# Sliding-window attention and an MLP on one core: a mask built on VectorE, key chunks shared by two query blocks, and a reordered, repacked load of the first batch

## The chip, the core and the metric

The kernel runs on one core of a Trainium2 chip. The metric is the device time of one execution in microseconds (us), as the median of several runs; smaller is better.

## What is computed

The first stage is attention over 8 batches, 8 heads, 576 tokens and 64 values per head, where a token sees the tokens at most 32 away from it. The second stage is an MLP on the 4608 tokens, 512 wide, with 2048 hidden values.

```python
scores = scale * np.matmul(q, k.transpose(0, 1, 3, 2))
mask = np.abs(pos[:, None] - pos[None, :]) <= 32
scores = np.where(mask, scores, -1000000000.0)
attn = softmax(scores)
x = np.matmul(attn, v).transpose(0, 2, 1, 3).reshape(4608, 512)
h = x @ w_in                       # 512 -> 2048
g = h * (1.0 / (1.0 + np.exp(-1.702 * h)))
out = (g @ w_out).astype(np.float32)
```

## The kernel before

**Tiling.** The 4608 tokens are cut into 36 units of 128 query tokens, and two units make one tile `t` of 256 tokens for the MLP. For a unit `u`, `scores` (L230) makes two PSUM tiles `sc`, one for the even and one for the odd heads. Each unit needs 192 keys, that is three chunks of 64; each of its two blocks of 64 queries uses two of them. A product has 64 contracted values, 64 keys and 64 queries, so it fills one quarter of the array, and four different quarters follow one another: per head pair 2 blocks x 2 key halves x 2 (even, odd) = 8 products, 32 in a unit. ScalarE takes the exponential (L251). In the first four units the window is cut before that by `blind` (L222), which puts -30000 into `sc` with a product of the identity and the tile `neg`; later units multiply by a 0/1 mask on VectorE (`band`, L254). `values` (L265) multiplies by v with a column of ones, `norm` (L278) divides on VectorE (4 instructions), `x_T` (L289) transposes the result into `xT`, on TensorE in the first eight units and by a DMA later. A unit's second block needs v shifted by 64 tokens: `odd_v` (L163) makes that copy `vo` with two instructions, the second of which needs the first half of the next unit's v.

**MLP.** `layer1(t, d)` (L304) makes two of 16 hidden blocks (8 products 128x256, w_in first), and ScalarE takes the activation. Column quarter `c` of w_in serves `d` = 2c and 2c+1. The second layer follows in the window after (`layer2` for the first tiles, then `product`, `keep` and `result` with sums made by `g_sums` and `w_sums`).

**Order.** The schedule is manual: each engine executes its instructions in the order in which the Python code calls them, and only semaphores tie the engines together. `head` (L421) writes out the order of the first four units and of all first loads; `window` (L578) does the rest, one window of 14.6 us for each later pair of units.

**Loads.** k, q, v and the weights are 32-bit in DRAM and are cast on the way, so all but the first four loads are issued by GpSimd (POOL) on one queue, which the DMA engines serve in order. A load's issue also waits until the eighth load before it on this queue has landed. The first batch's k and q come in two parts, since a part is what is needed first: part A is tokens 0 to 319 (two head pairs raw through SP and ACT, the others by POOL), part B tokens 320 to 575. Part B lies on 64 partitions with 4 tokens of a head in a row of 1 KB of source; VectorE pairs two heads (`pair_heads`, L200), TensorE transposes 4 times per head pair, and VectorE (k) or ScalarE (q) copies the result into the rings `kT` and `qT` (`rows_T`, L186).

**The order of POOL's work before** is: ident; k and q of part A; `neg` (one memset, four selects); v of units 0, 1, 2; k and q of part B; v 3; half of v 4; four quarters of w_in; `odd_v` of units 2 and 3 (four copies); w_out 0 and 2; the mask (9 instructions); k and q of tokens 512 to 1023 ("batch 1" below); w_out 1; more v.

**The order of TensorE before**, after the part A transposes, is: scores 0 and 1; 3 junk products; values 0; 3 junk; x_T 0; 1 junk; values 1; 4 junk; x_T 1; blind 2 and 3; 1 junk; the part B transposes; scores 2 and 3; layer1(0,0); values 2; layer1(0,1); values 3; x_T 2; layer1(0,2); x_T 3; layer1(0,3); layer1(1,0) and on. The junk products (`keep_busy`, L414) write nothing that is used.

Of the kernel before, what the change touches and what calls it, by code (L numbers as in the profile page):

```python
# [16 lines left out]
BF16 = mybir.dt.bfloat16  # L17
F16 = mybir.dt.float16
AF = mybir.ActivationFunctionType
ALU = mybir.AluOpType  # L20

SQ = 64
JT = 4
NV = 8
RING = 1536


class _Kernel:
# [7 lines left out]
    def __init__(self, ctx, tc, q, k, v, w_in, w_out, out):  # L36
        self.tc, self.nc = tc, tc.nc
        self.q, self.k, self.v, self.w_in, self.w_out, self.out = q, k, v, w_in, w_out, out
        self.B, self.H, self.S, self.D = q.shape
        self.N = self.B * self.S  # L40
        self.DM = self.H * self.D
        self.DFF = w_in.shape[1]
        self.NK = self.DM // 128
        self.NFF = self.DFF // 128
        self.scale = 1.0 / (self.D ** 0.5)
        self.NU = self.N // 128
        self.NW = self.NU // 2

        def pool(name, bufs, **kw):
            return ctx.enter_context(tc.tile_pool(name=name, bufs=bufs, **kw))  # L50

        self.cst = pool("cst", 1)
        self.work = pool("work", 2)
        self.ps = pool("ps", 1, space=bass.MemoryType.PSUM)
        self.stage, self.paired = {}, set()
        self.span = {"A": (0, 320), "B": (320, 256)}
        self.xT, self.g, self.o_ps = {}, {}, {}
        self.p, self.acc, self.x, self.sc = {}, {}, {}, {}
        self.gs, self.part, self.o_sb = {}, {}, {}
# [94 lines left out]
            self.nc.sync.dma_start_transpose(dst[:, :, at:at + 128],  # L154
                                             self.stage[c, i][:, n].rearrange("p h d -> p (h d)"))

    def load_v(self, m, half=None):
        for i, (off, b, s, n) in enumerate(self.pieces(128 * m, 128)):
            if half in (None, i):
                self.nc.gpsimd.dma_start(self.ve[m % NV][off:off + n, :, :self.D],  # L160
                                         self.v[b, :, s:s + n, :].rearrange("h s d -> s h d"))

    def odd_v(self, m, eng):  # L163

# [21 lines left out]
    def rows_T(self, c, i, hp, kind, eng):  # L186
# [3 lines left out]
        self.cast(eng, dst[:, hp, at:at + size].rearrange("r (p j) -> r p j", j=JT),  # L190
                  tp[:, :, :size // JT].rearrange("r j p -> r p j"))

    def load_raw(self, c, hp, eng):

        lo, size = self.tokens("A")
        raw = self.stage[c, "raw", hp] = self.cst.tile([size // JT, 2, JT * self.D], F32, name=f"{c}_raw{hp}")
        src = {"q": self.q, "k": self.k}[c]
        eng.dma_start(raw, src[0, 2 * hp:2 * hp + 2, lo:lo + size, :].rearrange("h (p j) d -> p h (j d)", j=JT))
# [10 lines left out]

    def setup_neg(self):  # L210

        pool = self.nc.gpsimd
        self.neg = self.cst.tile([128, 2, SQ], BF16, name="neg")
        pool.memset(self.neg, 0.0)
        for b in range(2):
            for half in range(2):
                sign = 1 if half == b else -1
                ap = self.neg[64 * half:64 * half + 64, b, :]
                pool.affine_select(out=ap, in_=ap, compare_op=ALU.is_ge, fill=-30000.0, base=0,  # L219
                                   pattern=[[-sign, SQ]], channel_multiplier=sign)  # L220

    def blind(self, u):  # L222

# [6 lines left out]
    def scores(self, u):  # L230
        nc = self.nc
        seen = u not in self.sc
        if seen:
            self.sc[u] = [self.bank("a", [128, 8, SQ], F32, f"sc{eo}") for eo in range(2)]
        sc = self.sc.pop(u)
        n = 0
        for hp in range(4):
            for blk in range(2):
                k0 = (128 * u + 64 * blk) % RING
                q0 = (128 * u + 64 * blk + 32) % RING  # L240
                for half in range(2):
                    lo, at = 64 * half, k0 + 64 * (half ^ blk)
                    for eo in range(2):
                        r = slice(eo * 64, eo * 64 + 64)
                        nc.tensor.matmul(sc[eo][lo:lo + 64, 2 * hp + blk, :], self.kT[r, hp, at:at + 64],  # L245
                                         self.qT[r, hp, q0:q0 + SQ], start=(seen and n == 0),
                                         stop=(n == 7), skip_group_check=not seen)
                n += 1
        p = self.work.tile([128, 2, 8, SQ], BF16, name="p", tag="p", bufs=5)
        for eo in range(2):  # L250
            nc.scalar.activation(p[:, eo], sc[eo], AF.Exp, scale=self.scale)  # L251
        self.p[u] = p
# [168 lines left out]
    def head(self):  # L421

        nc, dve, act, pool = self.nc, self.nc.vector, self.nc.scalar, self.nc.gpsimd
# [4 lines left out]
        for c in "kq":  # L428
            self.load_heads("A", c, (4, 8))
        self.setup_neg()  # L430
        for m in range(3):
            self.load_v(m)
        for c in "kq":
            self.load_heads("B", c)
        self.load_v(3)
        self.load_v(4, 0)
        for c in range(4):
            self.load_w_in(c)
        self.odd_v(2, pool)
        self.odd_v(3, pool)  # L440
        for c in (0, 2):
            self.load_w_out(c)
        self.setup_mask()
        self.cut_mask()
        for c in "kq":
            self.load_heads(1, c)
        self.load_w_out(1)
        self.load_v(4, 1)
        for m in range(5, 7):
            self.load_v(m)  # L450
        self.load_w_out(3)
# [12 lines left out]
        self.scores(0)  # L464
        self.scores(1)
        self.odd_v(0, dve)
        self.odd_v(1, act)
        self.keep_busy(3, "h")
        self.values(0, "hh")
        self.norm(0)  # L470
        self.keep_busy(3, "o")
        self.x_T(0, "t", act)
        self.keep_busy(1, "o")
        self.values(1, "oa")
        self.norm(1)
        self.keep_busy(4, "a")
        self.x_T(1, "a", act)
        self.blind(2)
        self.blind(3)
        self.keep_busy(1, "h")  # L480
        for hp in range(4):
            self.pair_heads("k", "B", hp, dve)
        for hp in range(2):
            self.pair_heads("q", "B", hp, dve)
        for hp in range(4):
            self.rows_T("k", "B", hp, "htho"[hp], dve)
            if hp < 2:
                self.pair_heads("q", "B", hp + 2, dve)
            self.rows_T("q", "B", hp, "hoth"[hp], act)
        self.scores(2)  # L490
        self.scores(3)
        self.layer1(0, 0)
        self.values(2)
        self.norm(2)
        self.layer1(0, 1)
        self.values(3)
        self.norm(3)
        self.x_T(2, "t")
# [274 lines left out]
```

## Time and profile before

| what | value |
|---|---|
| median of 5 runs | 294.05 us (293.83 to 295.7) |
| the profiled execution | 293.83 us, span of its instructions 292.1 us |
| TensorE busy | 285.6 us, 98% of the span |
| VectorE, ScalarE, GpSimd busy | 187.7, 185.2, 104.3 us |
| time before the first layer1 product starts its unbroken run (L313) | 18.69 us |
| 128x256 products of layer 1, one after another | 109 ns each |
| scores of two units, 64 products | 0.67 us |

The profile counts time from the first instruction. A line of a timeline or of the chain begins with start and length in us. The chain of work that ended last is followed back from the end, at each step to what released the step. TensorE's products overlap, so one product's length (193 ns for a scores product) is not the time between two of them.

The trace also has the moment at which a load's semaphore was complete, for most of the first loads:

```
load               issued us    landed us
k A, q A           1.57, 2.36   6.58, 7.39
v 0, 1, 2          4.35 to 7.17 -, 9.78, 10.80
k B, q B           7.15, 7.83   -, 14.72
v 3, half of v 4   8.51, 9.38   15.78, 16.12
w_in 0, 1, 2, 3    10.05 to 13.1  18.45, -, 23.53, 26.08
w_out 2            18.57        31.16
k batch 1 (last)   21.99        33.86
```

### The profile page before, as it was taken

To read this page: it belongs to the slowest core of one execution; us is meant where nothing else is said; L and a number is where in the kernel's file an instruction comes from. 1 tells how busy PE (TensorE), PEld (TensorE's weight loads), DVE (VectorE), ACT (ScalarE), POOL (GpSimd) and SP (SyncE) were. 2 spreads that over 40 slices of the span, in tenths; PEclk is the share of its full clock that TensorE was granted. 3 is DMA by queue.
4 is the path that set the end of the run, shared out by engine and by line. 5 is a ranking of instruction groups with operands and counts; after the bars stand their busy time and mean duration, and the time that the engine had idled before them with its cause. 6 is when DMAs were issued, how large, how long until landed. Compare 5 with 4: busy or idle time off the path is not lost.

```text
span 292.1 us, 9542 instructions
## 1 busy us (share of the span) xinstructions
PE 285.6 (98%) x4020; PEld 235.0 (80%) x4020; DVE 187.7 (64%) x552; ACT 185.2 (63%) x306; POOL 104.3 (36%) x146
## 2 busy tenths in 40 slices
PE   8989999999999999999999999999999999999995
PEld 3568764866888888888888888887888888888884
DVE  2663367688485858585858585857585858583353
ACT  4677547685766767676767676766575757575330
POOL 8875534989634444342424443332000000000000
PEclk9999999999999999999999999999999999999999
DMA  8999999999999999999999999999925330303012
GB/s 145 153 206 206 200 184 166 172 135 151 163 156 173 155 143 156 160 139 199 126 165 128 179 107 151 142 162 130 162 43 143 41 105 8 104 10 103 2 72 72
DMA packets 145291, 38.83 MB, mean 133 GB/s; under 512 B 129888, under 2 KB 140896, under 8 KB 145248
## 3 DMA queue, kind: packets, MB, share of 16 engines
q0 software_dynamic: 97696, 18.16, 85.1%
q1 hardware_dynamic: 47104, 19.67, 40.1%
q8 instruction: 31, 0.51, 0.7%
q10 hardware_dynamic: 448, 0.39, 0.5%
q14 instruction: 12, 0.10, 0.1%
HBM read 36.96 MB, written 9.44 MB: 159 GB/s over the span
## 4 chain that ended last, share of the span: by engine, by line
PE 93%; DVE 2%; DMA 2%; POOL 1%; issue 1%; ACT 0%; POOLq 0%; DVEq 0%
PE h_ps L313 43%; PE o_ps L375 32%; PE o_ps L325 7%; PE pv L273 4%; PE sc L245 4%; DMA ve<-in_v_dram 2%; PE tp L179 1%; PE tp L300 1%; DVE x L285 1%; PE sc L227 0%; POOL ve L160 0%; DVE o_sb L393 0%; POOL neg L219 0%; DVE kT L105 0%; ACT qT L105 0%
## 5 line engine op out<-in xcount | busy, mean ns | idle before, releaser
L313 PE MATMUL h_ps<-xT,w_in_sb 128*128 128x256 bf16 x1152 | 135.1, 273 | 0.0
L315 ACT ACTIVATE g<-h_ps 128x512 f16<-128x512 f32 x144 | 85.5, 595 | 73.9 <-PE h_ps L313 72.6
L313 PEld LDWEIGHTS <-w_in_sb 128*128 128x128 bf16 x1152 | 112.1, 98 | 13.3
L160 POOL DMA_DIRECT2D ve<-in_v_dram x40 | 34.0, 856 | 78.0 <-PE pv L273 57.9
L375 PEld LDWEIGHTS <-gs 128*128 128x128 f16 x480 | 45.8, 98 | 5.8
L375 PE MATMUL o_ps<-w_sum,gs 128*128 128x256 f16 x360 | 44.3, 273 | 0.0
L251 ACT ACTIVATE p<-sc 128x512 bf16<-128x512 f32 x72 | 37.2, 603 | 2.7 <-PE sc L245 2.5
L375 PEld LDWEIGHTS <-g 128*128 128x128 f16 x360 | 34.2, 98 | 4.5 <-ACT g L315 0.2
L352 DVE TENSOR_TENSOR gs<-g 128x512 f16<-128x512 f16 x30 | 12.7, 425 | 38.3 <-ACT g L315 38.3
L285 DVE TENSOR_TENSOR x<-pv,rec 128x256 bf16<-128x256 f32 x72 | 30.6, 425 | 2.5
L375 PE MATMUL o_ps<-w_out_sb,g 128*128 128x256 f16 x240 | 29.1, 273 | 0.0
L105 DVE COPY part<-o_ps 128x256 f32<-128x256 f32 x45 | 19.1, 424 | 13.3 <-PE o_ps L375 11.8
L393 DVE TENSOR_TENSOR o_sb<-o_ps,part 128x256 f32<-128x256 f32 x45 | 19.0, 423 | 12.0 <-PE o_ps L375 11.4
L147 POOL DMA_DIRECT2D qs<-in_q_dram x27 | 22.9, 869 | 5.7 <-DMA ks<-in_k_dram 4.3
L262 DVE TENSOR_TENSOR p<-p,mask 128x512 bf16<-128x512 bf16 x64 | 24.5, 424 | 0.6 <-ACT p L251 0.5
L147 POOL DMA_DIRECT2D ks<-in_k_dram x27 | 22.8, 860 | 2.1 <-DMA ve<-in_v_dram 2.1
L325 PE MATMUL o_ps<-w_out_sb,g 128*128 128x512 f16 x96 | 23.2, 380 | 0.0
L105 DVE COPY vo<-ve 64x528 bf16<-64x528 bf16 x65 | 20.7, 318 | 2.8 <-DMA ve<-in_v_dram 1.4
L251 ACT ACT_TABLE_LOAD x15 | 19.2, 1283 | 0.3
L412 ACT ACT_TABLE_LOAD x15 | 19.2, 1283 | 0.3
L284 DVE RECIPROCAL rec<-pv 128x4 f32<-128x4 f32 x72 | 12.6, 175 | 10.3 <-PE pv L273 10.3
L273 PEld LDWEIGHTS <-p 128*64 128x64 bf16 x576 | 11.2, 110 | 6.6 <-DVE p L262 3.2
(70 smaller groups left out, 246.8 us busy)
## 6 DMA issues: line engine op xcount, KB each, us to landing
out_dram<-o_sb SPq DMA_DIRECT2D x34, 256.0 KB, 6.1
ve<-in_v_dram POOLq DMA_DIRECT2D x32, 128.0 KB, 6.0
ks<-in_k_dram POOLq DMA_DIRECT2D x22, 128.0 KB, 7.9
qs<-in_q_dram POOLq DMA_DIRECT2D x22, 128.0 KB, 9.7
w_in_sb<-in_moe_w_in_dram POOLq DMA_DIRECT2D x4, 512.0 KB, 12.0
w_out_sb<-in_moe_w_out_dram POOLq DMA_DIRECT2D x4, 512.0 KB, 12.6
ve<-in_v_dram POOLq DMA_DIRECT2D x8, 64.0 KB, 5.6
ks<-in_k_dram POOLq DMA_DIRECT2D x7, 64.0 KB, 6.2
```

What stands on the lines that cost most here:

```text
L105: (eng.copy if eng is self.nc.scalar else eng.tensor_copy)(out, in_)
L147: self.nc.gpsimd.dma_start(self.stage[key][off:off + m, n], src[b, :, s:s + m, :].rearrange("h s d -> s h d"))
L160: self.nc.gpsimd.dma_start(self.ve[m % NV][off:off + n, :, :self.D], self.v[b, :, s:s + n, :].rearrange("h s d -> s h d"))
L251: nc.scalar.activation(p[:, eo], sc[eo], AF.Exp, scale=self.scale)
L262: self.nc.vector.tensor_mul(pv, pv, msk.to_broadcast([128, 4, 2, SQ]))
L273: nc.tensor.matmul(acc[half][blk * 64:blk * 64 + 64, hh, :], p[:, h % 2, h // 2 * 2 + blk, :], vt[:, h, :D + 1], start=(hh == 0), stop=(hh ...
L285: nc.vector.tensor_mul(x[:, hs, :], acc[half][:, :, :D], rec[:, hs, :].to_broadcast([128, 4, D]))
L313: nc.tensor.matmul(hps[:, i, :], self.w_in_sb[:, kr, ff * 128:(ff + 1) * 128], self.xT[t][:, kr, :], start=(i == 0 and kr == 0), stop=(i = ...
L315: nc.scalar.activation(self.g[t][:, ffs[0]:ffs[1] + 1:ffs[1] - ffs[0], :], hps, AF.Gelu_apprx_sigmoid)
L325: nc.tensor.matmul(o_ps, self.g[t][:, ff, s * 128:(s + 1) * 128], self.w_out_sb[:, ff, :], start=(ff == 0), stop=(ff == self.NFF - 1))
L375: nc.tensor.matmul(self.part[t, key], x, y, start=(first and k == 0), stop=(k == 7), skip_group_check=True)
L412: self.nc.scalar.activation(self.spark, self.spark, AF.Gelu_apprx_sigmoid)
```

## The change

- `neg` is made by 14 small VectorE instructions (running sums of the identity, then scale and shift) in place of POOL's 5.
- v 2 and v 4 are loaded in halves of 64 tokens; only the first half of v 2 stands ahead of part B.
- Part B is loaded by `load_rest`: rows of 8 tokens of a head (2 KB of source), heads 0 to 3 on partitions 0 to 31 and heads 4 to 7 on 32 to 63, so four loads in place of two. `rest_T` transposes it without pairing, 32 products of 64x64 for k and 32 for q into one PSUM tile each, and two copies of 128x512 per tile, one by ScalarE and one by VectorE. The built program makes the second copy of each tile wait for the first.
- The first quarter of w_in is issued behind part B, ahead of the rest of v 2, of v 3 and of v 4.
- `odd_v` of unit 1 goes from ScalarE to VectorE, those of units 2 and 3 from POOL to VectorE, behind scores 3.
- `scores`: the middle key chunk takes both query blocks in one product of 128 columns, so a head pair has 6 products, 24 in a unit. The columns streamed are as many as before.
- Order: x_T 0 and 1 now stand behind values 1, between the part B transposes of k and of q; blind 3 stands behind those; layer1(0,1) stands ahead of values 2; there are 5 junk products fewer; the loads of batch 1 are issued ahead of the mask.

```diff
+    def load_rest(self, c):
+        rest = self.stage[c, "B"] = self.work.tile([128, 4, 8 * self.D], BF16, name=c + "s", tag=c + "s", bufs=3)
+        src = {"q": self.q, "k": self.k}[c]
+        for g in range(2):
+            self.nc.gpsimd.dma_start(rest[32 * g:32 * g + 32],
+                                     src[0, 4 * g:4 * g + 4, 320:576, :].rearrange("h (p j) d -> p h (j d)", j=8))
+    def rest_T(self, c, kind, engs):
+        tp = self.bank(kind, [128, 2, 8, 64], BF16, "tp")
+        for n in range(4):
+            for j in range(8):
+                self.nc.tensor.transpose(tp[64 * (n % 2):64 * (n % 2) + 64, n // 2, j, :],
+                                         self.stage[c, "B"][:64, n, j * self.D:(j + 1) * self.D], self.ident[:64, :64])
+        dst = {"q": self.qT, "k": self.kT}[c]
+        for g in range(2):
+            self.cast(engs[g], dst[:, 2 * g:2 * g + 2, 320:576].rearrange("r h (p j) -> r h p j", j=8),
+                      tp[:, :, :, 32 * g:32 * g + 32].rearrange("r h j p -> r h p j"))
...
-        pool.memset(self.neg, 0.0)
-        for b in range(2):
-            for half in range(2):
-                sign = 1 if half == b else -1
-                ap = self.neg[64 * half:64 * half + 64, b, :]
-                pool.affine_select(out=ap, in_=ap, compare_op=ALU.is_ge, fill=-30000.0, base=0,
-                                   pattern=[[-sign, SQ]], channel_multiplier=sign)
+        for i in range(2):
+            dve.memset(tri[i][:, :pad], 0.0)
+        for rows in (lo, hi):
+            dve.tensor_copy(tri[0][rows, pad:], self.ident[rows, rows])
+        for i in range(6):
+            a, b = tri[i % 2], tri[(i + 1) % 2]
+            dve.tensor_add(b[:, pad:], a[:, pad:], a[:, pad - (1 << i):pad + SQ - (1 << i)])
+        for rows, b in ((lo, 0), (hi, 1)):
+            dve.tensor_scalar(out=self.neg[rows, b, :], in0=tri[0][rows, pad - 1:pad + SQ - 1], scalar1=-30000.0,
+                              scalar2=None, op0=ALU.mult)
+            dve.tensor_scalar(out=self.neg[rows, 1 - b, :], in0=tri[0][rows, pad:], scalar1=30000.0, scalar2=-30000.0,
+                              op0=ALU.mult, op1=ALU.add)
...
+            for chunks in ((1, 0), (2,)):
+                for eo in range(2):
+                    r = slice(eo * 64, eo * 64 + 64)
+                    for c in chunks:
+                        lo = 64 * (c % 2)
+                        b0, n = (1, 1) if c == 2 else (0, 1 + c)
+                        nc.tensor.matmul(sc[eo][lo:lo + 64, 2 * hp + b0:2 * hp + b0 + n, :],
+                                         self.kT[r, hp, k0 + 64 * c:k0 + 64 * c + 64],
+                                         self.qT[r, hp, q0 + SQ * b0:q0 + SQ * (b0 + n)],
...
-        for m in range(3):
+        for m in range(2):
             self.load_v(m)
-        for c in "kq":
-            self.load_heads("B", c)
+        self.load_v(2, 0, 64)
+        for c in "kq":
+            self.load_rest(c)
+        self.load_w_in(0)
+        self.load_v(2, 64)
         self.load_v(3)
-        self.load_v(4, 0)
-        for c in range(4):
+        self.load_v(4, 0, 64)
+        for c in range(1, 4):
             self.load_w_in(c)
-        self.odd_v(2, pool)
-        self.odd_v(3, pool)
         for c in (0, 2):
             self.load_w_out(c)
+        for c in "kq":
+            self.load_heads(1, c)
         self.setup_mask()
         self.cut_mask()
-        for c in "kq":
-            self.load_heads(1, c)
...
-        self.odd_v(1, act)
+        self.odd_v(1, dve)
         self.keep_busy(3, "h")
         self.values(0, "hh")
         self.norm(0)
-        self.keep_busy(3, "o")
-        self.x_T(0, "t", act)
-        self.keep_busy(1, "o")
+        self.keep_busy(2, "o")
         self.values(1, "oa")
         self.norm(1)
-        self.keep_busy(4, "a")
-        self.x_T(1, "a", act)
         self.blind(2)
+        self.rest_T("k", "t", (act, dve))
+        self.x_T(0, "h", act)
+        self.x_T(1, "h", act)
+        self.rest_T("q", "o", (dve, act))
         self.blind(3)
-        self.keep_busy(1, "h")
...
+        self.keep_busy(2, "h")
         self.scores(2)
         self.scores(3)
+        self.odd_v(2, dve)
+        self.odd_v(3, dve)
         self.layer1(0, 0)
+        self.layer1(0, 1)
         self.values(2)
         self.norm(2)
-        self.layer1(0, 1)
         self.values(3)
```

## The prediction, before the run

> **What bounds the kernel now.** I read the busy line first, then the chain of work that ended last in order of time, then TensorE's timeline around the scores, then the landings of the first loads.
>
> ```profile
> PE 285.6 (98%) x4020; PEld 235.0 (80%) x4020; DVE 187.7 (64%) x552; ACT 185.2 (63%) x306; POOL 104.3 (36%) x146
> ...
> PE 93%; DVE 2%; DMA 2%; POOL 1%; issue 1%; ACT 0%; POOLq 0%; DVEq 0%
> ```
>
> TensorE is the bound, and only its share of the chain (93%) leaves room. The chain says where:
>
> ```profile
> 4.16 0.24 POOL neg L219
> 4.40 0.95 POOL ve L160
> 5.34 4.44 DMA ve<-in_v_dram
> 9.87 0.36 DVE vo L105
> ...
> 13.57 0.44 DVE x L285
> ...
> 15.86 0.42 DVE kT L105
> 16.29 0.38 DVE qc L105
> ...
> 17.73 0.38 ACT qT L105
> ...
> 18.69 0.98 PE h_ps L313 x8
> 19.67 0.38 PE pv L273 x16
> 20.04 0.98 PE h_ps L313 x8
> 21.02 0.38 PE pv L273 x16
> 21.40 0.33 PE tp L300 x4
> ...
> 22.85 11.35 PE h_ps L313 x104
> ```
>
> All other engines' shares lie ahead of 18.69 us (and in the last 5 us, which the change leaves alone). From there TensorE runs without a gap, but for one of 0.55 us at 201 that the chain puts down to issue. So there are two questions: how much earlier does this run start, less the gaps that open in it; and does the scores' own time, repeated in every window, shrink?
>
> ```profile
> 211.01 0.67 PE sc L245 x64
> ```
>
> **What the Trainium skill says.**
> 1. "TensorE: Matmul & The Clock Gate", Back-to-back issue gap: a warm product costs N/2.4 + 2.5 ns. The trace agrees: 109 ns for 256 columns.
> 2. "TensorEngine Tiling (Array Packing)", Key Properties: tiles of the array work independently. In a scores block four products start 3 to 4 ns apart, the next four 32 ns after the first four, in the same quarters: 32 ns per product and quarter, for 29 by the formula.
> 3. "SBUF — State Buffer", Door 1: 64 partitions starting at 0 take a load no faster than 32 do (196 and 189 GB/s for 1 MiB). The trace has 64 partitions only: k and q B, 512 KB together, landed 3.92 us after v 2 (10.80 to 14.72), 134 GB/s, against some 205 for w_in.
> 4. "VectorE: DVE Perf Modes", The TRN2 errata: a two-input bf16 operation has about 150 cycles of fixed cost. The trace agrees: 128x512 takes 424 ns, 267 of them for two elements a cycle at 0.96 GHz, so 157 ns are fixed.
>
> **The change, part by part.**
>
> *neg.* POOL loses 2.99 to 4.35: 1.36 us ahead of v 0. VectorE gains 14 operations. Six dependent adds cost 157 + 33 = 190 ns and about 40 for the hand-over (reciprocal to product: 0.22 start to start for 0.18): 1.4 us. The other eight at 70 (memset row) to 200 ns: about 1.0. From 1.5 to about 3.9 us, under the wait for k_raw, which lands at 4.42. Upper end: 14 x 0.3 = 4.2 us, then the first kc copy is 1.3 late, the second (5.39) 0.6: S below moves by 0.6. Lower end: nothing.
>
> *Loads.* v packets were partly limited by issue (v 1 and 2 land 3.5 to 3.6 us after their issue ends), so 1.36 us of issue is worth about 0.4 at v 1, as part A holds the engines until 7.39. Half of v 2 no longer stands ahead (0.5). Twice the row, half the packets: for the 512 KB I take 3.0 us, between 2.5 (w_in's rate) and 3.92 (no gain; page 3 gives no reason for a loss from 32 partitions). Four issues of about 0.55 cost POOL 0.8 more than two of 0.7, covered by the queue in front. So q B lands at 14.72 - 0.4 - 0.5 - 0.9 = 12.9 (12.2 to 13.8), k B near 11.4. Then w_in 0 after its 2.33: 15.2 (18.45 before); v 2's rest, v 3, half of v 4 (0.4 + 1.06 + 0.4): 17.1 (16.12 before); w_in 1 19.6.
>
> *odd_v 1 from ScalarE to VectorE.* It took 11.14 to 12.42 on ScalarE, and values 1 waited (12.41). On VectorE it is done by 10.4, before norm 0's first wait ends (10.6). Values 1 now wait for the exponential (ends 11.12): 11.2. Norm 1 ends at 13.0, by norm 0's end 11.8 + 1.2; before 13.99.
>
> *Part B.* VectorE loses eight pairing copies (0.28 to 0.36 each) and four kT copies (0.41), ScalarE four qT copies (0.37); they gain four 128x512 copies, by the rows of batch 1 0.69 on VectorE, 0.58 on ScalarE, in a series because each second one waits. TensorE: 32 transposes in one quarter after another, eight in each, so 32 ns each (row of page 2): 1.0 us; twice that if weight loads are exposed when only one quarter works, half if quarters overlap. Chain: blind 2 ends 12.0; k transposes end 13.15 (193 ns behind the last start); ScalarE kT 13.73; VectorE kT 14.5; meanwhile x_T 0, x_T 1 (x ready 13.0), q transposes 13.5 to 14.65; VectorE qT 15.4; ScalarE qT 16.05; blind 3 and junk lie under this. The last two head pairs of scores 2 and all of scores 3: 0.13 + 0.26 + 0.17 for the ends. Layer1(0,0) starts at S = 16.65; w_in 0 is there with 1.4 to spare. Before: 18.69.
>
> *layer1(0,1) ahead of values 2.* This opens a gap. Before, norm 2 lay under it. Now values 2 start at v = S + 1.95; norm 2's halves end at v + 1.0 and v + 1.55 (19.60, 21.15 before), values 3 at v + 0.76, so x_T 2 stalls 0.8; norm 3 ends at v + 2.67, layer1(0,2) covers all but 0.1 of it. Layer1(0,3) starts at S + 4.85 = 21.5, for 22.85 before. **Gain of the head: 1.4 us.**
>
> *odd_v 2 and 3 on VectorE.* 4 x 0.35, behind v 4's landing at 17.1: done 17.5, values 2 at 18.6. Norm 2 is queued behind; a landing after 18.2 adds to the stall one to one. POOL is freed by 2.6 us, worth nothing: its next issues wait for landings.
>
> *Batch 1, mask, w_out.* The next place where TensorE needs a load is batch 1's q: pairing started at 36.67, its transposes were due at 37.87, 0.7 us to spare. TensorE comes 1.4 earlier, the queue 1.2 to 1.8: no stall. The mask is due beyond 43 us. *Junk products* filled waits: nothing.
>
> *Scores.* 288 products fewer, columns unchanged. Per head pair a low quarter still runs two 64-column products, 2 x 32 = 64 ns, a high one a 128-column product, 56. The low quarters bind: 64 as before. At best the low ones reach 29 each: 58, or 45 ns in each pair of units. I take 20 ns x 16 pairs = 0.3 us; ends 0 and 0.75, and a rival for the case that products count.
>
> Sum against the profiled execution: 293.83 (span 292.1 and 1.73 around it) - 1.4 - 0.3 = 292.1; the median lies 0.22 above it: **292.3**.
>
> **The rivals.**
> - *Products, not columns, cost.* If a scores block goes with its number (0.67 x 48/64 = 0.50), 16 pairs give 2.7: 289.9. For it: 10.5 ns a product. Against: the groups of four at 32 ns.
> - *The head's gain is mostly eaten.* Transposes at twice the price: +1.0 for k, +1.0 for q, partly under copies, S near 18.0; or q B no sooner than 14.72, with S near 17.8. The head's gain is then 0.0 to 0.3, and with the scores' 0.3 the time 293.6. For it: four copies and two transpose blocks in one series have no cover. Against: weight loads were hidden in each quarter before.
> - *Slower: packing onto 32 partitions halves the rate of part B.* 7.8 us for 3.92: q B lands at 13.8 + 3.9 = 17.7. Once q B is last, S lies 3.1 behind it (transposes 1.2, two copies 1.4 with their waits, scores 0.5): 20.8, 2.8 past the break-even S = 18.0 (22.85 - 4.85). With the scores' 0.3: 296.5. It decides from a landing of q B at 14.9. For it: 64 partitions were already slow. Against: page 3.
> - That the change doesn't do what it says can't be the case in the order of instructions, which I read in the built program.
>
> **How the numbers follow.** Forecast 0.55 (291.2 to 293.0 by the bounds of S +-0.4, scores 0 to 0.75); eaten 0.25 (293.0 to 294.2); products cost 0.12; slower 0.08. Range 290.7 to 294.2 leaves out most of the last two, 0.18. A measurement of this kernel tells about 0.5% (1.47 us) from no change; the limit 292.58 lies inside the forecast's own case, so two thirds of it (0.38) and the 0.12 count as faster: 0.50; same 0.43; slower 0.07.
>
> **What would show it.** q B landing at 12.2 to 13.8; first layer1 at 16.3 to 17.1; kT, kT, qT, qT copies in a row between 13.1 and 16.1; a stall of TensorE of 0.7 to 0.9 ahead of x_T 2 on VectorE's x; a scores block of 0.62 to 0.67; no wait at batch 1's q. Wrong if a block takes 0.5, if transposes come at 60 ns, or if the first layer1 waits for w_in.

## The result and the profile after

The changed kernel takes 292.21 us in the median (291.53 to 294.43), the kernel before 294.18 in the runs beside it: a ratio of 0.9934, 95% interval 0.992 to 0.9947. A second series gave 0.9922 (0.9895 to 0.9949). The forecast was 292.3. The profiled execution took 292.86 us with a span of 291.2; that of the second series took 291.8 with 290.1. In 28 of the 115 executions of the kernel before that were taken beside the experiments, and in 1 of 32 of the changed kernel, the mean granted clock was 0.994 or less and the time some 1.5 to 2.3 us longer; among the others the medians are 293.9 us before and 292.1 and 291.8 after, so the gain doesn't rest on it.

First two lines of the page after, busy times and the chain's shares by engine:

```profile
PE 284.0 (98%) x3759; PEld 234.1 (80%) x3759; DVE 192.4 (66%) x562; ACT 183.9 (63%) x302; POOL 101.6 (35%) x140
...
PE 89%; DMA 5%; DVE 3%; ACT 1%; issue 1%; POOL 0%; POOLq 0%; DVEq 0%
```

TensorE is the bound as before, with 1.6 us less busy time. Then the chain of work that ended last, in order of time (start, length, what), in the head of the changed kernel:

```profile
2.35 5.49 DMA qs<-in_q_dram
...
7.88 0.35 PE tp L181 x8
...
9.40 1.08 ACT p L277 x2
...
11.54 0.45 PE pv L299 x16
11.98 0.54 PE sc L253 x2
12.52 0.82 PE tp L205 x32
13.34 0.55 PE tp L326 x8
13.90 0.82 PE tp L205 x32
14.72 0.54 PE sc L253 x2
15.26 0.43 issue
15.69 0.59 PE junk L444 x2
16.28 0.63 PE sc L270 x33
16.91 1.85 PE h_ps L339 x16
...
19.26 0.42 DVE x L311
...
20.58 0.87 PE h_ps L339 x8
21.45 0.22 PE tp L326 x4
21.68 4.37 PE h_ps L339 x40
```

Three things are to be seen. From 11.54 to 16.91 the chain is TensorE's own order, but for 0.43 us that the profile puts down to `issue`: no load of part B stands in it, neither k B nor q B. The first layer1 product starts at 16.91, 1.78 earlier than before; the run behind x_T 3 starts at 21.68, 1.17 earlier than before's 22.85, because x_T 2 now waits for VectorE (19.02 to 20.30). And the chain begins with q A, which landed at 7.84 in this execution and at 7.39 in the one before the change, though its issue is the same; in the second profile of the changed kernel it landed at 7.46, layer1 began at 16.47 and the run behind x_T 3 at 21.25, 1.60 earlier than before.

A block of scores, again from the chain:

```profile
209.86 0.63 PE sc L270 x32
```

(32 is the number of products that the chain kept of the 48.) It was 0.67 before.

How much earlier than before TensorE reaches a given scores block shows where the gain is made and lost:

```
scores block before at   lead, changed   lead, second profile
17.63 (scores 2, 3)      1.42            1.85
42.82                    1.17            1.60
65.14                    1.25            1.69
78.38                    0.68            1.38
107.86                   0.78            1.48
122.47                   0.25            1.51
180.98                   0.33            1.60
195.59                   0.37            1.42
210.94                   1.15            2.20
254.78                   1.26            2.32
```

Against this one profile of the kernel before, the head gives 1.2 to 1.6, each window adds 0.03 to 0.05 (the scores), and single gaps take or give the rest: one at 65 us in both profiles of the changed kernel, one at 111 us in the first only (TensorE waits for a DMA transpose that took 9.75 us), and the 0.55 us of `issue` at 201 us which the prediction saw in the kernel before; what this last one most likely is comes at the end of the experiments.

The gap at 65 us was in no part of the prediction. The chain there, in the first profile:

```profile
60.30 0.82 DVE vo L105
...
61.15 0.65 DVE vo L105
...
61.82 0.67 DVE vo L105
...
62.52 0.85 DVE vo L105
...
64.28 0.84 DVE vo L105
65.13 0.25 DVE p L288
...
65.38 0.42 DVE p L288
...
65.84 0.41 PE pv L299 x14
```

Six shifted copies of v (units 7 to 9), 0.30 to 0.69 us each before and 2.4 in all, took 4.8 in all. The mask of unit 7 stands behind them on VectorE, values 7 behind the mask, and TensorE waited 0.6.

### The profile page after: what moved, and what is told of

Read it like the earlier page. It is cut to its first block, busy times and chain, and to the rows that moved or that the text cites. A ratio compares the mean times of both kernels' runs of the same rounds, so it can differ in the third digit from the quotient of the medians.

```text
span 291.2 us, 9011 instructions
## 1 busy us (share of the span) xinstructions
PE 284.0 (98%) x3759; PEld 234.1 (80%) x3759; DVE 192.4 (66%) x562; ACT 183.9 (63%) x302; POOL 101.6 (35%) x140
## 4 chain that ended last, share of the span: by engine, by line
PE 89%; DMA 5%; DVE 3%; ACT 1%; issue 1%; POOL 0%; POOLq 0%; DVEq 0%
PE h_ps L339 41%; PE o_ps L401 31%; PE o_ps L351 6%; PE pv L299 4%; PE sc L270 3%; DMA xT<-x 3%; DMA qs<-in_q_dram 2%; DVE vo L105 1%; PE tp L178 1%; PE tp L326 1%; PE tp L205 1%; PE junk L444 0%; ACT p L277 0%; PE sc L253 0%; DVE o_sb L419 0%
## 5 line engine op out<-in xcount | busy, mean ns | idle before, releaser
L105 DVE COPY vo<-ve 64x528 bf16<-64x528 bf16 x71 | 24.9, 350 | 5.0 <-DMA ve<-in_v_dram 3.4
## 6 DMA issues: line engine op xcount, KB each, us to landing
w_out_sb<-in_moe_w_out_dram POOLq DMA_DIRECT2D x4, 512.0 KB, 13.9
```

The source lines that it names most:

```text
L105: (eng.copy if eng is self.nc.scalar else eng.tensor_copy)(out, in_)
```

## The experiments

Ratios are to runs of the kernel before beside them on the same chip. The changed kernel's own, 0.9934 and 0.9922, are the mark for those that start from it.

### Which part of the gain is the scores

**The kernel before with the new `scores` alone** (e1).

> The kernel before with the new scores alone (6 products per head pair in place of 8). Theory: the quarters bind, not the number of products, so a block of two units goes from 0.67 us only to about 0.63 as in the profile after; 16 blocks give 0.6 us, time 293.5, ratio 0.998. Rival 1, products cost: a block takes 0.50, time 291.5, ratio 0.991. Rival 2, columns alone cost: block 0.67, ratio 1.000. If the scores made the whole gain of the change, the ratio would be 0.9934.

Measured: 293.16 us, 0.997 (0.9954 to 0.9986): the theory's 0.998 lies within the interval, both rivals outside.

**The changed kernel with the old `scores`** (e2).

> The changed kernel with the old scores: what the head alone brings. Theory: blocks of 0.67 us, the head's gain of 1.2 to 1.3 us stays (first unbroken layer1 run, behind x_T 3, at 21.7 us as after), time 292.9, ratio 0.9957. Rival, the head's gain is eaten later by stalls that the profile after shows at 62 to 66 and at 111 us: ratio 0.998 or more.

Measured: 293.71 us, 0.9973 (0.9953 to 0.9992); the interval holds both the theory's 0.9957 and the rival's 0.998. In its profile the run behind x_T 3 starts at 23.40, later than before, behind waits on issue of 0.8 us at 14.77 and 1.23 at 20.52, so that this one execution had lost the head's gain. By the times the scores bring about 0.9 us alone and 1.1 on top of the rest, each with some 0.5 to 0.7 us of uncertainty; both hold the 0.64 us that 16 blocks at 0.63 for 0.67 make. The prediction took 0.3, and the products rival 2.7. Both are off, the rival far more. The parts add up: 0.997 x 0.9973 = 0.9943, beside 0.9934 for the whole.

### The earlier issue

**The changed kernel with `neg` on GpSimd** (e4), as before:

```diff
-        dve.memset(...)   # 14 instructions on VectorE
+        pool.memset(self.neg, 0.0)
+        pool.affine_select(...)   # four times
```

> The changed kernel with neg made by POOL again, so that all v loads are issued 1.36 us later. Theory of the prediction: v 1, v 2 and part B land 0.4 later, q B at about 13.75, the first layer1 0.25 later: time 292.5, ratio 0.9943. Rival, from the profile after: the earlier v issue brought nothing (v 1 landed at 9.90, before 9.78) and its packets stood between those of part A, whose q landed at 7.84 instead of 7.39; then with POOL's neg q A lands at 7.4 again, scores 0 start 0.3 earlier, the first layer1 0.1 to 0.3 earlier: time 292.0, ratio 0.9925.

Measured: 293.7 us, 0.9971 (0.9951 to 0.9992): 1.1 us of the gain are gone (0.5 to 1.7 by this interval). The chain of that kernel:

```profile
4.14 0.24 POOL neg L238
4.38 2.50 POOL ve L159 x3
6.88 1.09 POOL ks L197 x2
...
8.46 6.85 DMA qs<-in_q_dram
...
15.36 0.91 PE tp L205 x32
```

Here the chain does run through GpSimd's `neg` and the load of q B: it landed at 15.32, and the transposes of q, due near 13.9, waited for it.

**The kernel before with `neg` on VectorE and nothing else** (e10).

> The kernel before with only the neg mask moved from GpSimd to VectorE. The prediction's term: 0.4 us at the landing of q B (14.3 for 14.72), the first layer1 product 0.4 earlier (18.3), the time 293.8, ratio 0.9985. Rival, from the changed kernel with neg put back on GpSimd (q B at 15.3 in place of 13.35, 1.1 us slower): the earlier issue lets the packets of v and of part B follow without a break, q B lands near 13.2, the first layer1 product starts 0.8 to 1.3 earlier (17.4 to 17.9), 293.1, ratio 0.9965.

Measured: 293.73 us, 1.0002 (0.9981 to 1.0024): no gain shows in the time. The rival's 0.9965 lies outside the interval; the 0.4 us of the prediction (0.9985) lies within it and isn't excluded. Yet q B landed at 13.59, 1.1 before the 14.72 of the kernel before. VectorE's and GpSimd's timelines of e10 tell where it went (start, length, engine, line; x is the number of instructions):

```profile
14.12 1.31 DVE L105 COPY kc<-ks 64x512 bf16<-64x512 bf16 x4
15.36 0.91 DVE L105 COPY qc<-qs 64x512 bf16<-64x512 bf16 x2
16.19 0.40 DVE L105 COPY kT<-tp 128x256 bf16<-128x256 bf16 x1
16.52 1.06 DVE L105 COPY qc<-qs 64x512 bf16<-64x512 bf16 x1
```

```profile
14.63 2.17 POOL L105 COPY vo<-ve 64x528 bf16<-64x528 bf16 x3 [2.20 <-DMA ve<-in_v_dram]
```

v 3 landed earlier as well, so GpSimd's copies for unit 2 and 3 ran from 14.63 instead of 15.90, right across VectorE's pairing copies. These took 1.31 us for kc and 1.06 for one qc, where before they took 0.88 and 0.46. The three copies that grew longest ended 0.09 to 0.15 us behind the end of a GpSimd instruction (15.29 and 15.43, 16.12 and 16.27, 17.49 and 17.58). The first layer1 product came at 19.68, 1.0 later than before (0.2 of it was there at norm 1, which ended that much later). Besides, pairing starts behind norm 1, at 13.91 before and 14.12 here, so that an earlier q B had little to give in this execution of the old order: the chain of the kernel before has no load of part B in it either. That isn't so in every execution. e1 issues the same loads at the same times, and in its profile q B landed at 15.88, VectorE waited 1.12 us for it, and the chain leads through GpSimd's `neg`:

```profile
7.77 8.11 DMA qs<-in_q_dram
...
15.90 0.49 DVE qc L105 x2
```

Together: in the old order the earlier issue is worth nothing that these runs can show (0.6 us at most, by the interval of e10), since GpSimd's copies take back a part of what it brings; in the new order, where q is due at 13.9, it is worth 1.1 us. It is a condition of the gain more than a part that can be added.

### The packing

**The changed kernel with part B in rows of 4 tokens** (e6), 1 KB of source on 64 partitions, two loads instead of four, the same 32 transposes:

```diff
-        for g in range(2):
-            self.nc.gpsimd.dma_start(rest[32 * g:32 * g + 32], ... "h (p j) d -> p h (j d)", j=8))
+        self.nc.gpsimd.dma_start(rest[:64], ... "h (p j) d -> p h (j d)", j=4))
```

> The changed kernel with part B of k and of q loaded by one load each on 64 partitions, in rows of 4 tokens (1 KB of source), as before, and the same number of transposes and copies. If larger rows are worth what the prediction gave them (0.9 us at q B): q B lands at 14.3 to 14.5 instead of 13.35, the first layer1 product starts 0.6 later, near 17.5, 292.8, ratio 0.9955. Rival, the earlier issue brought all of it and the packing little: q B at 13.3 to 13.6, 292.2, ratio 0.9934.

Measured: 291.93 us, 0.9913 (0.988 to 0.9945), not slower than the changed kernel: the rival. The time alone isn't a clean sign, since this edit also changes the quarter of the array every four transposes instead of every eight, and each set of 32 took 0.18 us less. q B landed at 12.98. The landings of the first loads shift between executions, so I compare the stretch from the landing of v 2, or of its half, to that of q B:

```
kernel                        neg on    rows    v 2      q B     stretch
before (whole v 2 first)      GpSimd    1 KB    10.80    14.72   3.92
e1 (whole v 2 first)          GpSimd    1 KB    11.36    15.88   4.52
e4                            GpSimd    2 KB    10.76    15.32   4.56
e10 (whole v 2 first)         VectorE   1 KB    10.74    13.59   2.85
e6                            VectorE   1 KB     9.57    12.98   3.41
e11 (below)                   VectorE   1 KB    10.43    13.45   3.02
changed                       VectorE   2 KB    10.54    13.35   2.81
changed, second profile       VectorE   2 KB     9.99    12.74   2.75
e5 (below)                    VectorE   2 KB    10.87    13.53   2.66
e12 (below)                   VectorE   2 KB    10.40    13.37   2.97
```

Once the issue is early the 512 KB take 2.85 to 3.41 us in rows of 1 KB and 2.66 to 2.97 in rows of 2 KB: the larger rows bring between nothing and 0.75 us. With `neg` on GpSimd they take 3.9 to 4.6 us in either. So what separates the stretches is the issue. From 6 to 10 us the DMA engines moved 112 to 143 GB/s in each microsecond in the kernel before, e1 and e4, and 152 to 200 in the changed kernel, its second profile and e10.

### The place of w_in

**The changed kernel with w_in 0 behind v 3 and half of v 4** (e5).

> The changed kernel with the first quarter of w_in issued behind the rest of v 2, v 3 and the half of v 4 (where the kernel before had it). If the early issue of w_in is part of the gain: it lands near 17.6 instead of 15.91, layer1(0,0) starts at 17.65 instead of 16.91, and the time is 0.7 us above the changed kernel's 292.2: 292.9, ratio 0.9955 to the kernel before. Rival, its place doesn't matter because part B sets the start, or because a stall behind takes the difference up: layer1(0,0) at 16.9, or later with the stall ahead of x_T 2 gone; 292.2, ratio 0.9934.

Measured: 292.67 us, 0.9952 (0.9934 to 0.997), the time expected of the first theory, though the interval overlaps that of the changed kernel, so that the time alone doesn't decide. TensorE's timeline names the wait:

```profile
17.20 1.92 PE L339 MATMUL h_ps<-xT,w_in_sb 128*128 128x256 bf16 x16 [0.45 <-DMA w_in_sb<-in_moe_w_in_dram]
```

w_in 0 landed at 17.15, and the first layer1 product waited 0.45 for it.

### The stall ahead of x_T 2

**The changed kernel with layer1(0,1) behind values 2 and norm 2** (e3), the order of before.

> The changed kernel with layer1(0,1) put back behind values 2 and norm 2. Theory: x_T 2 no longer waits 1.1 us for norm 2; values 2 start at about 17.9 instead of 18.7, norm 2 is then held by the odd values of unit 3 (ready 18.55), so x_T 2 stalls some 0.3 and the run behind x_T 3 starts at 21.15 instead of 21.68: 0.5 us faster than the changed kernel, time 291.7, ratio 0.9917. Rival, values 2 and norm 2 are held by the late landing of v 3 and v 4 as much as by their place: no gain, 292.2, ratio 0.9934.

Measured: 292.43 us, 0.9937 (0.9913 to 0.9962): the same as the changed kernel. The stall goes, but the chain then holds another wait:

```profile
12.03 8.61 DMA w_in_sb<-in_moe_w_in_dram
20.63 0.04 issue
20.68 1.05 PE h_ps L339 x8
```

layer1(0,2) waits for w_in 1, which landed at 20.63 there and at 20.06 in the changed kernel, where layer1(0,2) starts at 20.58. The stall costs nothing that a better order of these steps alone would give back. What TensorE waits for here also moves between executions: the chain leads through w_in 1 in e7 as well (landed at 20.24), and through v 3 in e6 (17.15).

### The series of copies

**The changed kernel with two PSUM tiles for each transposed result** (e8), so that the two engines copy side by side:

```diff
-        tp = self.bank(kind, [128, 2, 8, 64], BF16, "tp")
-        for n in range(4):
+        for i in range(2):
+            tp = self.bank(kinds[i], [128, 8, 64], BF16, "tp")
+            for n in (2 * i, 2 * i + 1):
```

> The changed kernel with each of the two transposed part B results in two tiles of PSUM in place of one, so that ScalarE's and VectorE's copies run side by side and the first begins after 16 of 32 transposes. If the series of copies (kT, kT, qT, qT from 13.38 to 16.07) sets the first layer1 product: the last copy ends near 15.45, layer1(0,0) starts at 16.3 instead of 16.91, and the run behind x_T 3 starts 0.5 earlier, 21.15 for 21.68: 291.7, ratio 0.9917. Rival, the landing of the second quarter of w_in (20.06) and VectorE's norm 2 hold what follows: layer1(0,0) at 16.3, but the run behind x_T 3 within 0.15 of 21.68; 292.1, ratio 0.9931.

Measured: 292.09 us, 0.9919 (0.9889 to 0.9949). In the trace it did what was expected: from the start of k's transposes (12.45, as in the changed kernel to 0.07) the chain runs on TensorE without a wait, and layer1(0,0) and the run behind x_T 3 are 0.5 earlier than in the first profile:

```profile
15.78 0.63 PE sc L270 x32
16.41 1.85 PE h_ps L339 x16
...
21.18 2.84 PE h_ps L339 x26
```

Not all of the 0.5 us is the copies': the 0.43 us of `issue` ahead of the junk products, which stands in both profiles of the changed kernel (0.43 and 0.37), is missing here. From the start of k's transposes to layer1(0,0) it is 3.96 us in e8, 4.39 and 4.33 in the two profiles of the changed kernel, and 4.23 in e7 (next), which has the copies in series and no such wait. So by these profiles the series is worth about 0.27 us, and the wait the rest. The time can't tell either from none.

### The six slow copies

**The changed kernel with these copies as a maximum of v with itself** (e7), a two-input operation with the same result:

```diff
-        self.cast(eng, vo[64:128], self.ve[m % NV][64:128])
+        self.nc.vector.tensor_max(vo[64:128], ve[64:128], ve[64:128])
```

> The changed kernel, with the six shifted copies of v of units 7, 8 and 9 on VectorE made by a two-input operation (the maximum of v with itself, the same values) in place of a copy. If the copies take twice as long there because VectorE's copies and GpSimd's issues of loads exclude each other, the two-input form isn't held up: six of about 0.46 are 2.8 us in place of 4.83, the mask of unit 7 starts near 63.1 in place of 65.05, TensorE's gap of 0.6 at 65 is gone, and the time is 291.6, ratio 0.9914. Rival, the copies are slow for another reason (their data, or GpSimd holds up any VectorE work): the six still take 4 to 5 us, the gap stays, 292.2, ratio 0.9934.

VectorE's timeline of e7, and the chain there:

```profile
60.17 0.43 DVE L173 TENSOR_TENSOR vo<-ve 64x528 bf16<-64x528 bf16 x1
...
62.43 0.42 DVE L174 TENSOR_TENSOR vo<-ve 64x528 bf16<-64x528 bf16 x1
63.08 0.91 DVE L294 TENSOR_TENSOR p<-p,mask 128x512 bf16<-128x512 bf16 x2 [0.23 <-ACT p L283]
```

```profile
64.21 0.97 PE o_ps L357 x4
65.17 0.38 PE pv L305 x16
```

Six take 2.7 us, the mask starts at 63.08 and waits for ScalarE, and TensorE has no gap. GpSimd was issuing loads in the same order, but for a pause from 60.28 to 60.70; in e11 and e12 (below) it issued without a break, and the six took 0.43 each again. So the copies were slow for their form, beside GpSimd's issues. The Trainium skill, "SBUF — State Buffer", Who interferes with whom, says that a VectorE copy in a two-port mode and GpSimd exclude each other, that an instruction holds the shared ports to its end, and that a two-input operation has no such mode, though with both inputs in SBUF it contends with a GpSimd instruction that reads SBUF. The traces agree on the copies, and show no delay of the two-input form: 0.43 us each under GpSimd's issues, and 0.65 to 0.87 for copies which take 0.30 when left alone. In the changed kernel each copy ended about 0.22 us behind the start of an issue of GpSimd's (60.91, 61.59, 62.26, 63.14, 64.01; copies end at 61.12, 61.80, 62.49, 63.37, 64.25): they took turns. But an issue doesn't hold the copies off for all its length, as the page's rule would have it: in the kernel before a copy of 0.30 us (62.53 to 62.83) ran inside an issue (62.42 to 63.11). Here the measurement decides.

The time doesn't show it: 292.03 us, 0.9939 (0.9908 to 0.997). **The changed kernel again** (e9) was to tell whether the gap belongs to it:

> The changed kernel once more, unchanged, beside the three below. 292.2, ratio 0.9934. If TensorE's gap of 0.6 at 65 us belongs to the changed kernel, the six copies of v there take 4.8 us again and the gap is there again; if it depends on how GpSimd's issues fall in one execution (in two of the last four kernels the copies took 2.8 us), it may be gone, and its removal is worth less than 0.6 in the median.

Measured: 291.79 us, 0.9922 (0.9895 to 0.9949); the copies took 4.57 us and the gap was 0.33. Across the eleven profiles with the copies as they were the six take from 1.9 to 4.8 us; in e5 and e6 GpSimd paused for 0.4 and 0.8 in their midst, and from there on a copy took 0.29 to 0.44, also under the issues that followed. So the gap depends on how GpSimd's issues fall in an execution, and what its removal is worth in the median stays open: under 0.6 us.

### All of it

**The changed kernel with two tiles, with transposes that change the quarter of the array at each step, with the two-input copies, and with 1 KB rows** (e11), **and the same with 2 KB rows** (e12):

```diff
-            for n in (2 * i, 2 * i + 1):
-                for j in range(8):
+            for j in range(8):
+                for n in (2 * i, 2 * i + 1):
```

> The changed kernel with three edits: part B in rows of 1 KB on 64 partitions (as in the run with that edit alone), two tiles of PSUM for each transposed result, with the transposes alternating between the quarters of the array one by one, and the two-input form for the six copies of v at 60 us. If the series of copies and the gap at 65 both count in the median: layer1(0,0) near 16.0 and the run behind x_T 3 near 20.9, no gap at 65: 291.2, ratio 0.990. Rival, w_in's second quarter (landing about 19.5 to 20.2) and norm 2 hold the run and the gap at 65 is rare: 291.8, ratio 0.992. In the trace: 32 transposes in 0.5 us if two quarters work at once, 0.65 to 0.82 if a quarter's change costs nothing.

> The same as the run before it, but with part B in rows of 2 KB on twice 32 partitions, as in the changed kernel. The prediction's term for the packing would make it faster by up to 0.6 us (q B 0.6 earlier); if q B isn't what the transposes wait for (they start behind values 1 and the mask product, near 13.1 to 13.8), the two agree within 0.3 us.

Measured: e11 291.52 us, 0.9901 (0.9877 to 0.9925); e12 292.1 us, 0.9911 (0.9882 to 0.994), beside 0.9922 for the changed kernel on the same chip. Rows of 1 and 2 KB agree, as the second expectation has it for a load that nothing waits for, though these intervals can't tell 0.6 us from nothing. e11 is the fastest of all, but its interval overlaps that of the changed kernel, so that it beats the change isn't shown; against the kernel before it is 0.75% to 1.2% faster. In its profile the head ran into a wait that the profile puts down to issue:

```profile
12.48 0.62 PE tp L211 x32
...
15.08 0.94 issue
16.02 0.70 PE sc L274 x32
16.72 1.85 PE h_ps L343 x16
```

The transposes take 0.62 us for 0.82, and what the side by side copies had opened went into these 0.94 us (the second junk product has no record and lies within them).

The profile names no cause for such waits, but the traces tell more. Below are TensorE's recorded instructions (products and weight loads) up to the wait, and the end of the last 16 KB packet before it on the DMA queue that the profile calls `instruction`:

```
kernel    waits ahead of   instructions so far     packet ended   wait ended
changed   junk             449                     14.09          15.69
e2        transpose of q   449                     14.14          15.58
e2        values 3         705 = 449 + 256         20.43          21.75
e6        junk             449                     13.40          14.93
e11       scores 2         448                     14.21          16.02
before    values           5825 = 449 + 21 x 256   200.25         201.88
```

Whatever the instruction is, the waits stand at one count or whole multiples of 256 behind it, to within three (profiles lack some records), and each ends 1.3 to 1.8 us behind such a packet. There are 31 of these packets for 8095 instructions of TensorE before and 29 for 7577 after, one for some 261. So TensorE most likely waited for its next instructions. No run changes the number or place of instructions to test this.

## Why the prediction was right

**The sum.** 292.3 was forecast, 292.21 measured. The head was to give 1.4 us and gave 1.17 and 1.60 in the two profiles. The scores were to give 0.3 and gave about 0.6. The gaps at 65 and 111 us, which no step of the prediction has, took it back in the first profile. By the table of leads it had 1.17 at 42.8 us, lost 0.57 and 0.53 across the two gaps, won 0.78 where the kernel before had its wait at 201 us, gained 0.03 to 0.05 in most other windows, and had 1.26 at 254.8. The end of the last stores took another 0.27 (3.56 us behind TensorE's last product, for 3.29 before), and the spans differ by 0.97; in the second profile they differ by 2.03. The agreement to 0.1 us is thus partly luck.

**Part B and the start S.** Forecast 16.65, measured 16.91 and 16.47. The copies, forecast as kT 13.15, kT, qT, and qT to 16.05, ran from 13.38 to 16.07. The transposes came 23 ns from start to start, not 32. No run takes the order of x_T, the transposes without pairing, or odd_v 1 on VectorE out by itself, so their shares of the head's gain are read from the chains (values 1, for instance, start at 11.54 for 12.41) and not tested.

**From S to the run behind x_T 3.** Forecast 4.85 us, measured 4.77 and 4.78 in the two profiles: the stall which layer1(0,1) opens was costed rightly. That its removal gains nothing (e3) was not foreseen; w_in 1, forecast at 19.6, landed at 20.06.

**neg on VectorE.** Forecast from 1.5 to 3.9 us under the wait for k_raw; it ran from 1.37 to 4.2, hidden. The six adds took 0.19 us each with 0.03 between them, close to the 0.19 and 0.04 of the sum.

**The loads.** q B was forecast at 12.9 (12.2 to 13.8) and landed at 13.35 and 12.74. The two terms behind it were mis-sized against each other. "1.36 us of issue is worth about 0.4": it moved q B by 1.1 (e10, 14.72 to 13.59; 2.3 from e1's 15.88) and by 2.0 (e4, 15.32 to 13.35). The packing, put at 0.9, moved it by 0 to 0.75. The reason for the error is in the prediction's own row: 134 GB/s for 64 partitions was read as the price of rows and partitions, when the same rows on the same partitions took 2.85 to 3.41 us for 3.92 once their issue was earlier, and the larger rows took 4.56 when it was late. That q B landed within the range is two errors which offset each other. Why the DMA engines move less from 6 to 10 us when the issue is late isn't settled.

**odd_v 2 and 3.** "POOL is freed by 2.6 us, worth nothing" holds for GpSimd's queue and misses VectorE: e10 shows what those copies do to VectorE's when they meet. A version of the change with them left on GpSimd wasn't tried.

**The scores.** The low quarters were to bind at 64 ns per head pair with 20 ns per pair of units to gain. The first half is right: a head pair takes 63 ns before and after, by the starts of its products. The block went from 0.67 to 0.63, 40 ns, and these lie at its end: the last product starts 550 ns into the block before, 505 after.

**The rivals.** A block of 0.63 us rules the products rival out (0.50), the landing of q B rules out the half rate (17.7), and a head 1.2 to 1.6 shorter isn't eaten. The point that rival named, q B at 14.9, was near: with `neg` on GpSimd it landed at 15.3, the first layer1 product came 2.9 behind it (3.1 in the forecast), and more than half of the gain was gone.

## What to carry to other kernels

Ask of an earlier load who is waiting for it in the order at hand: the same 1.36 us of issue was worth 1.1 us in the new order and nothing that could be measured in the old one, so parts of a change have to be valued together. Don't read a transfer's rate as the price of its layout before its issue is known to have been early. Where GpSimd issues loads back to back, look at VectorE's copies beside it, and try a two-input form for those with a consumer behind them. Where a wait is put down to issue, count the engine's instructions up to it before looking for a missing semaphore or load.

## What the hardware showed that was not expected

- A VectorE copy of 64x528 took 0.30 us alone and, where it took turns with GpSimd's issues of loads, 0.65 to 0.87; the two-input form took 0.43 under these issues.
- From the first to the last start, 32 transposes of 64x64 took 0.70 us with the quarter changed every eight, 0.52 with it changed every four (e6), and 0.50 to 0.62 with it changed every time (e11, e12): two quarters by turns do not halve it, and every four is as good as every time.
- With all data there, TensorE waited 0.43 us (changed kernel, 15.26), 0.94 (e11, 15.08) and 1.23 (e2, 20.52) at places in its own instructions which lie whole multiples of 256 apart (to within three), each time 1.3 to 1.8 us behind the end of a 16 KB packet of the instruction queue.
- The landing of q A, issued at 2.35 in every kernel, moved between 7.2 and 8.2 us; where the chain starts with it, the head moved with it (first layer1 product at 16.91 with 7.84, at 16.47 with 7.46).
